# Windowed attention feeding an MoE layer: k of the later batches transposed by DMA, bulk loads tied to product slots, first steps reordered

## The chip, the cores and the metric

One core of a Trainium2 chip runs the whole program. The metric is the device time of one execution in microseconds. The kernel before was run six times: median 354.45 us, lowest 354.02, highest 355.26.

## The reference

Attention over a causal sliding window of 64 keys, for 8 batches of 8 heads with 576 positions of 64 numbers, and then a two-layer block over all 4608 tokens:

```python
scores = scale * np.matmul(q, k.transpose(0, 1, 3, 2))
mask = (rel >= 0) & (rel < window)          # rel = query position - key position
attn = softmax(np.where(mask, scores, -1e9))
attn_out = np.matmul(attn, v)
x = attn_out.transpose(0, 2, 1, 3).reshape(4608, 512)
h = x @ w_in                                 # 512 -> 2048
g = h - np.tanh(h)
out = g @ w_out                              # 2048 -> 512
```

q, k, v and the two weights come as float32, out is float32. The kernel multiplies in bfloat16 and accumulates in float32.

## The kernel before

**Two kinds of work on one in-order TensorE.** The MoE block runs over 9 chunks of 512 tokens. For each chunk `hp_mm` makes 16 tiles of the hidden layer (4 matmuls each, m = 0 to 15), ScalarE takes the tanh, VectorE subtracts (`g_sub`) into gT, and `yp_mm` makes the output from gT and w_out in 16 steps of 4 matmuls, 16 slots later (`LAG`). A slot is one `hp_mm` and one `yp_mm`; it is counted in two half-slots h: an even h holds the hidden product, an odd h the output product. After each group of four output steps `y_out` copies the result out of PSUM on ScalarE and stores it by SyncE. Between these products the attention is placed, pair of heads by pair of heads: g = 4 b + pr is pair pr (0 to 3) of batch b.

**The steps of one pair.** `cast` turns q or k of the pair, which were loaded with 96 groups of six positions on the partitions, into a row layout (GpSimd for most pairs). `tr` transposes the rows on TensorE, six 96x96 blocks each for q and k, into PSUM bank 3 (k of early pairs into bank 2), and copies the result into qT or kT (two buffers each, g modulo 2): q in two halves, by ScalarE and VectorE in the steady part, k in one copy on ScalarE. `scores` makes 9 blocks of 128 keys x 128 columns in three groups of three, each followed by an exp on ScalarE into PT; `masking` multiplies by the mask on VectorE (batches 0 and 1 add the mask by an extra matmul instead); `pv` multiplies by the values in vw; `norm` divides by the row sums on VectorE into xs. When the four pairs of a batch are done, x is transposed into xT, the operand of the MoE product: by TensorE for batches 0 to 2 (`x_tr`), by a transposing DMA on SyncE's queue from batch 3 on (`x_dma`, L251 to L259).

**The values** are loaded (`load_v_all`), cast by GpSimd into vb (`cast_v`, one pair of heads at a time), copied by nine small DMAs per batch from vb into the upper half of vw (`keys_v`, 65 KB each), and shifted into its lower half (`shift_v`, by DMA, or by VectorE for batches 0 and 1). vb is one buffer: a batch's casts wait until the copies of the batch before have landed.

**The loads** of whole batches (`load_all` for q and k, `load_v_all`) are issued by GpSimd, 576 KB each as written, with a cast to bfloat16 on the way; some of batch 0 go pair by pair, on the queues of GpSimd, SyncE or ScalarE (`load`). The weights go on GpSimd's queue too: w_in in three blocks (two of 512 KB, one of 1 MB, `load_w_in`), w_out in four (`load_w_out`).

**What sets the order.** The kernel writes every queue's order out by hand. `PLAN` maps a half-slot h to a script of short steps that `play` issues in that order: `q0a` loads q of pair 0 on ScalarE's queue, `r` does the same for k, `V1`, `K1`, `Q1` load batch 1, `a` and `b` cast q and k, `v` and `d` load and cast values, `k00s` is copy 0 of batch 0's values on SyncE, `z` the shift, `E` and `F` transpose q and k, `R40` is score group 0 of pair 4, `P` the value products with their norm, `M` the mask, `X` x's transpose, `w` and `o` the weight blocks, `n`, `i`, `m` constants. A last letter names the engine (p GpSimd, a ScalarE, v VectorE, s SyncE). The script at -1 is all that comes before the first MoE product. From pair 12 on a loop (L395 to L419) places each step at a half-slot worked out from a (the pair's) and s (the batch's); steps of one half-slot follow the product of that half-slot. Each engine then works through its own list in order, waiting by semaphores; SyncE's list holds value copies, shifts, x's transposes and the output stores, GpSimd's the loads and the casts.

Of the kernel before, what the change touches and what calls it, by code (L numbers as in the profile page):

```python
# [15 lines left out]
def kernel(  # L16
# [26 lines left out]
    const = ctx.enter_context(tc.tile_pool(name="const", bufs=1))  # L43
    qk_pool = ctx.enter_context(tc.tile_pool(name="qk", bufs=2))
    all_pool = ctx.enter_context(tc.tile_pool(name="all", bufs=2))
# [3 lines left out]
    xt_pool = ctx.enter_context(tc.tile_pool(name="xt", bufs=3))  # L49
    g_pool = ctx.enter_context(tc.tile_pool(name="g", bufs=2))  # L50
    psum = ctx.enter_context(tc.tile_pool(name="psum", bufs=1, space=PSUM))

# [3 lines left out]

    ident = const.tile([128, 128], BF16, name="ident")
    seen = const.tile([64, 128], BF16, name="seen")
    mask = ps[:, 5, 480:512].bitcast(BF16)
# [11 lines left out]
    kT = [const.tile([128, 64 + S], BF16, name=f"kt{i}") for i in range(NR)]  # L71
    qT = [const.tile([128, 2, S], BF16, name=f"qt{i}") for i in range(NR)]
    xs = [const.tile([128, NJ, NP, D], BF16, name=f"xs{i}") for i in range(2)]

# [8 lines left out]
    def load(g, n, eng):  # L83

        b, pr = divmod(g, NP)
        if eng is nc.gpsimd:
            if (b, n) not in whole:
                whole[b, n] = all_pool.tile([P, H, E * D], BF16, tag=n, name=n + "all")
            t = whole[b, n][:, pr::NP]
        else:  # L90
            t = qk_pool.tile([P, 2, E * D], F32, tag=n + "f", name=n + "f")
        eng.dma_start(out=t, in_=(q if n == "q" else k)[b, pr::NP].rearrange("h (p e) d -> p h (e d)", e=E))
        stage[g, n] = t

    def load_all(b, n):

        t = all_pool.tile([P, H, E * D], BF16, tag=n, name=n + "all")
        nc.gpsimd.dma_start(out=t, in_=(q if n == "q" else k)[b].rearrange("h (p e) d -> p h (e d)", e=E))
        for pr in range(NP):
            stage[b * NP + pr, n] = t[:, pr::NP]  # L100

    def cast(g, n, eng=nc.gpsimd):
# [59 lines left out]
    def more_constants():  # L162
        nc.vector.memset(qT[1], 0.0)
        nc.vector.memset(kT[1][:, 0:64], 0.0)
        for i in range(2):
            nc.vector.memset(vw[i][0:64, 0], 0.0)

# [25 lines left out]
    def tr(g, which, bank, *engs):  # L193
# [9 lines left out]
        else:  # L203
            move(engs[0], kT[g % NR][:, 64:].rearrange("c (p e) -> c p e", e=E), t)

    def scores(g, grp, bank):
        sp = ps[:, bank, 0:384].rearrange("p (i q) -> p i q", i=3)
        for i in range(3):
            j = 3 * grp + i
            nc.tensor.matmul(sp[:, i, :], kT[g % NR][:, 64 * j:64 * j + 128],  # L210
                             qT[g % NR][:, :, 64 * j:64 * j + 64], start=True, stop=g >= 2 * NP)
            if g < 2 * NP:
                nc.tensor.matmul(sp[:, i, :], ident, hide.rearrange("p h t -> p (h t)"), start=False, stop=True)
# [86 lines left out]
    def at(h, *fn):  # L300
        items.setdefault(h, []).append(fn)
# [13 lines left out]
    def play(script):  # L315
        for step in script.split():
# [50 lines left out]
        -1: """  # L367
            q0a r0s i a0v v00 v02 v03 d02a d00v b0a v01 q1a E0vv r1p d01v r2p m d03p b1v F0a
            k00s q3p k08a a1v R01 F1v R02 E1vv b2a k01p k02a k04a q2p k05s V1 R00 K1 k03s Q1 a2v
            n k06s F2a R10 k07s z0v R12 a3p r3s E2aa P0 d11p d13p w0 R11 w1 E3aa R22 b3a R21  # L370
            b5p w2 Q2 P1 K2 R20 d10p a5p F3v d12a k17s a4p P2 k16s R31 k10s b4p X001v V2 a7p
            k18s R30 b7p o2 k12s k13s X000a R32 b6p P3 o3 k15a X010v X011a E4vv""",
        0: "F4a",
        10: "a6v o0 R40 a9p aAp E5aa k14s b8p F5v a8p R42",
        12: "k11s d20p d22p R41 F6a d21p d23p z1v k25s k27s E6aa R50 P4",
        15: "b9p R52 o1 k24p k22s k20s R51 R61 F7a P5 R62 E7aa",
        19: "R60 F8a k23s R71 P6 k21p k28s X100a k26s R70",
        20: "R72 bBp bAp E8vv",
        23: "X101a P7 z2s R80 E9aa",
        24: "R81",  # L380
        26: "F9a R82 X111a X110a",
        31: "R90 EAvv",
        35: "R92 FAa R91 M8 aBp FBv M9",
        41: "RA2 P9",
        45: "P8 EBaa RA0",
        50: "RA1 X200a MA RB2 RB1 X201v PA RB0",
        56: "MB PB",
# [7 lines left out]
    for g in range(3 * NP, B * NP):  # L395
        b, pr = divmod(g, NP)
        a = 8 * g - 48 - (0, 2, 4)[min(b - 3, 2)]
        s = 32 * b - (0, 2, 4)[min(b - 3, 2)]
        at(a - 7, cast, g, "q")
        at(a - 5, cast, g, "k")  # L400
        at(s - 72 + 5 * pr, cast_v, b, pr)
        at(a, tr, g, "q", 3, nc.scalar, nc.vector)
        at(a + 2, tr, g, "k", 3, nc.scalar)
        for i in range(3):
# [5 lines left out]
        if pr == NP - 1:  # L410
            at(a + 16, x_dma, b)
        for j in range(NJ):
            if pr == 0:
                at(s - 54 + j // 2, keys_v, b, j)
        if pr == 0:
            at(s - 78, load_v_all, b)
            at(s - 64, load_all, b, "q")
            at(s - 63, load_all, b, "k")
            at(s - 47, shift_v, b, 0, NJ - 1)  # L419

# [45 lines left out]
```

## Time and profile before

| what | value |
|---|---|
| median of six runs | 354.45 us |
| the profiled execution | 354.02 us, its span 352.1 us |
| first MoE product starts | 38.67 us |
| last matmul ends | 348.35 us |
| loads of whole batches, issue to landing, median | v 12.0, k 9.7, q 6.4 us |
| moved by DMA | 39.70 MB; read from HBM 36.70 MB, written 9.44 MB |
| x's transposes by DMA | 10, each 1.2 to 5.9 us on SyncE's queue |
| granted TensorE clock | 1.00 |

The profile is of one execution. Its span runs from the first to the last instruction, so some 1.9 us of the execution's time lie outside. "Busy" is time in which an engine executes; PE is TensorE, PEld its weight loads, DVE VectorE, ACT ScalarE, POOL GpSimd, SP SyncE; a name with q (ACTq, SPq) is the engine's sequencer, which issues DMAs. A busy row of the page cuts the span into 40 slices of 8.8 us and gives tenths. In a table by stretch each engine has its busy time and its number of instructions in brackets. A timeline line has start, duration, engine, code line, operation, output and input tiles, and in square brackets how long the engine had been idle and for what it waited.

### The profile page before, as it was taken

Reading aid. Unit: us, or ns where it says so; the run is one execution under the profiler, and the core shown is the slowest. Engines: PE = TensorE matmul, PEld = TensorE weight load, DVE = VectorE, ACT = ScalarE, POOL = GpSimd, SP = SyncE. Lnnn points to the kernel's source line nnn. Section 1 sums busy time; section 2 is a strip of 40 time slices with the busy share of each in tenths; the row PEclk is TensorE's granted clock in tenths of the full one; section 3 lists DMA queues with packets and bytes.
Section 4 is the critical chain, followed back from the end, with each engine's and each line's share of the span. In section 5 each row is a group of like instructions: output and inputs, shape, how many; then the busy total and the mean of one; then the engine's idle time right before and its main releaser. Section 6 shows DMA issues by size and latency. Waiting matters only on the chain.

```text
span 352.1 us, 5822 instructions
## 1 busy us (share of the span) xinstructions
PE 315.6 (90%) x2208; PEld 181.4 (52%) x2239; DVE 204.7 (58%) x322; ACT 195.9 (56%) x356; POOL 104.9 (30%) x138
## 2 busy tenths in 40 slices
PE   0538677999899999999999999999999999999995
PEld 0427356655556555555555555555555444444442
DVE  3617666776676667666667676776776333333400
ACT  3337477955766666666666666666654444444421
POOL 8709625516328318405520642110000000000000
PEclk9999999999999999999999999999999999999999
DMA  8898998749868569965963594244001400010011
GB/s 160 138 207 133 220 209 161 114 102 182 166 118 116 99 136 163 172 141 120 181 115 110 117 156 131 63 100 97 32 31 40 119 30 32 30 60 32 30 77 73
DMA packets 43764, 39.70 MB, mean 113 GB/s; under 512 B 15336, under 2 KB 37672, under 8 KB 43352
## 3 DMA queue, kind: packets, MB, share of 16 engines
q0 software_dynamic: 20432, 17.97, 34.6%
q1 hardware_dynamic: 22600, 20.50, 22.3%
q10 hardware_dynamic: 704, 0.86, 0.8%
q8 instruction: 17, 0.28, 0.3%
q14 instruction: 11, 0.09, 0.1%
HBM read 36.70 MB, written 9.44 MB: 131 GB/s over the span
## 4 chain that ended last, share of the span: by engine, by line
PE 74%; DMA 10%; ACT 5%; DVE 5%; POOL 3%; issue 2%; POOLq 0%; ACTq 0%; DVEq 0%
PE ps L287 33%; PE ps L267 31%; DMA vall<-in_v_dram 6%; DMA vw<-vb 4%; PE ps L224 4%; PE ps L210 3%; PE ps L197 3%; ACT th L271 2%; DVE xs L235 1%; DVE gT L277 1%; ACT pt L214 1%; POOL vb L81 1%; ACT qt L79 1%; POOL vall L112 1%; DVE qt L81 1%
## 5 line engine op out<-in xcount | busy, mean ns | idle before, releaser
L277 DVE TENSOR_TENSOR gT<-ps,th 128x512 bf16<-128x512 f32 x144 | 99.1, 691 | 87.7 <-ACT th L271 84.9
L267 PE MATMUL ps<-xT,wi 128*128 128x512 bf16 x576 | 147.5, 379 | 1.2 <-DVE gT L277 0.9
L287 PE MATMUL ps<-w_out_sb,gT 128*128 128x512 bf16 x545 | 139.9, 379 | 1.8 <-ACT ysb L292 0.2
L271 ACT ACTIVATE th<-ps 128x512 f32<-128x512 f32 x144 | 86.0, 598 | 80.7 <-PE ps L267 80.2
L267 PEld LDWEIGHTS <-wi 128*128 128x128 bf16 x576 | 60.9, 113 | 46.6 <-issue 2.4
L287 PEld LDWEIGHTS <-gT 128*128 128x128 bf16 x576 | 53.6, 98 | 54.1 <-issue 0.5
L214 ACT ACTIVATE pt<-ps 128x384 bf16<-128x384 f32 x96 | 47.0, 491 | 45.9 <-PE ps L210 31.4
L81 POOL COPY vb<-vall 72x1024 bf16<-72x1024 bf16 x28 | 29.3, 1058 | 72.0 <-DMA vw<-vb 51.1
L235 DVE TENSOR_TENSOR xs<-ps,rc 64x576 bf16<-64x576 f32 x64 | 48.3, 755 | 1.5
L210 PE MATMUL ps<-qt,kt 128*128 128x128 bf16 x288 | 36.5, 226 | 9.7 <-ACT pt L214 8.7
L224 PE MATMUL ps<-vw,pt 128*128 128x130 bf16 x288 | 29.6, 223 | 6.4 <-DVE vw L133 3.3
L224 PEld LDWEIGHTS <-pt 128*128 128x128 bf16 x288 | 22.1, 99 | 22.3 <-issue 5.1
L81 POOL COPY qb<-qall 96x768 bf16<-96x768 bf16 x28 | 23.9, 857 | 31.1 <-PE ps L197 16.0
L81 DVE COPY qt<-ps 64x576 bf16<-64x576 bf16 x30 | 22.7, 758 | 14.6 <-ACT qt L79 13.2
L210 PEld LDWEIGHTS <-kt 128*128 128x128 bf16 x288 | 24.6, 102 | 10.4 <-issue 2.4
L81 POOL COPY kb<-kall 96x768 bf16<-96x768 bf16 x28 | 23.2, 831 | 22.0 <-DMA kall<-in_k_dram 10.4
L292 ACT ACTIVATE ysb<-ps 128x512 f32<-128x512 f32 x36 | 21.5, 597 | 14.7 <-PE ps L287 14.7
L79 ACT ACTIVATE qt<-ps 64x576 bf16<-64x576 bf16 x34 | 21.6, 636 | 1.7 <-PE ps L197 1.6
L197 PE MATMUL ps<-ident,qb 96*128 96x96 bf16 x192 | 14.5, 215 | 6.6 <-DVE qb L81 6.2
L79 ACT ACTIVATE kt<-ps 128x576 bf16<-128x576 bf16 x28 | 18.1, 648 | 1.0 <-PE ps L197 1.0
L218 DVE TENSOR_TENSOR pt<-pt,ps 128x1152 bf16<-128x1152 bf16 x24 | 17.9, 744 | 0.4 <-ACT pt L214 0.4
L197 PE MATMUL ps<-ident,kb 96*128 96x96 bf16 x192 | 14.1, 212 | 3.8 <-ACT kb L79 2.8
(48 smaller groups left out, 117.9 us busy)
## 6 DMA issues: line engine op xcount, KB each, us to landing
out_dram<-ysb SPq DMA_DIRECT2D x36, 256.0 KB
vw<-vb SPq DMA_DIRECT2D x65, 65.0 KB
vall<-in_v_dram POOLq DMA_DIRECT2D x7, 576.0 KB, 12.0
kall<-in_k_dram POOLq DMA_DIRECT2D x7, 576.0 KB, 9.7
qall<-in_q_dram POOLq DMA_DIRECT2D x7, 576.0 KB, 6.4
vw<-vw SPq DMA_DIRECT2D x6, 520.0 KB
w_out_sb<-in_moe_w_out_dram POOLq DMA_DIRECT2D x4, 512.0 KB, 19.5
wi<-in_moe_w_in_dram POOLq DMA_DIRECT2D x2, 512.0 KB, 7.2
```

The source lines that it names most:

```text
L79: nc.scalar.activation(o, i, ACT.Copy)
L81: eng.tensor_copy(o, i)
L197: nc.tensor.transpose(tp[:, e, :], src[:, e, :], ident[:P, :P])
L210: nc.tensor.matmul(sp[:, i, :], kT[g % NR][:, 64 * j:64 * j + 128], qT[g % NR][:, :, 64 * j:64 * j + 64], start=True, stop=g >= 2 * NP)
L214: nc.scalar.activation(PT[g % NPT][:, 3 * grp:3 * grp + 3, :], sp, ACT.Exp, scale=scale)
L224: nc.tensor.matmul(ps[:, 5 + grp, 130 * i:130 * i + 130], PT[g % NPT][:, j, :], vw[b % 2][:, j, 2 * pr:2 * pr + 2, :], start=True, stop=True)
L235: nc.vector.tensor_tensor(xo[r, :, :, pr, :], ov[r, :, :, h, 0:D], rc[r].to_broadcast([64, 3, 3, 64]), ALU.mult)
L267: nc.tensor.matmul(hp, w_in_tile(ki, m), chunk_tile(c)[:, :, ki % 2, 64 * (ki // 2):64 * (ki // 2) + 64], start=(ki == 0), stop=(ki == 3))
L271: nc.scalar.activation(th, hp, ACT.Tanh)
L277: nc.vector.tensor_tensor(gT[c][:, m, :], hp, th, ALU.subtract)
L287: nc.tensor.matmul(yp, gT[c][:, m, s * 128:(s + 1) * 128], w_out_sb[:, m, :], start=(m == 0), stop=(m == M - 1))
L292: nc.scalar.activation(ysb, ps[:, yp_bank(c, s), :], ACT.Copy)
```

## The change

k of batches 4 to 7 is no longer transposed by TensorE. GpSimd casts two pairs into one tile (`cast2`), SyncE writes that tile to a buffer in HBM (`bounce`), and SyncE reads it back with a transposing DMA (`tr2`) into kT2, which `scores` reads from pair 16 on. q, k and v of these batches are loaded at half-slots of their own, each after a one-element GpSimd copy (`pace`) that reads gT of the slot before. Pair 12 on is placed 4 half-slots earlier than its plain place, where batch 3 stood at its plain place and batch 4 at 2 earlier. q is cast at a-5 instead of a-7, x's transposing DMA goes out at a+15 instead of a+16, the shift at s-45 instead of s-47. The float32 staging tiles of q and k share three buffers in place of two each. The scripts of `PLAN` are written in another order, in which some steps also change engines (of batch 1's value casts, for example, three go to VectorE and one to GpSimd, where GpSimd had three and ScalarE one), and of the loads k of batch 1 stands later, and k and q of batch 2 stand ahead of the last block of w_in. TensorE has 192 rows fewer (96 transposes and their weight loads).

```diff
-    qk_pool = ctx.enter_context(tc.tile_pool(name="qk", bufs=2))
+    qk_pool = ctx.enter_context(tc.tile_pool(name="qk", bufs=3))
...
+    kT2 = [const.tile([128, 2, 64 + S], BF16, name=f"kt2{i}") for i in range(2)]
...
+    def pace(h):
+
+        c, m = divmod(h // 2 - 1, M)
+        nc.gpsimd.tensor_copy(tick, gT[c][0:1, m, 0:1])
...
     def more_constants():
         nc.vector.memset(qT[1], 0.0)
         nc.vector.memset(kT[1][:, 0:64], 0.0)
+        for i in range(2):
+            nc.vector.memset(kT2[i][:, :, 0:64], 0.0)
...
+    def cast2(g, n):
+
+        if g % 2 == 0:
+            two[n, g // 2] = two_pool.tile([P, E, 2, 2, D], BF16, tag=n, name=n + "b2")
+        nc.gpsimd.tensor_copy(two[n, g // 2][:, :, g % 2].rearrange("p e h d -> p h e d"),
+                              stage.pop((g, n)).rearrange("p h (e d) -> p h e d", d=D))
+
+    def bounce(i, n):
+        t = dram.tile([S, 256], BF16, tag=n, name=n + "d")
+        nc.sync.dma_start(out=t.rearrange("(p e) c -> p (e c)", e=E),
+                          in_=two[n, i].rearrange("p e i h d -> p (e i h d)"))
+        two[n, i] = t
+
+    def tr2(i, n):
+        nc.sync.dma_start(out=kT2[i % 2][:, :, 64:], in_=two.pop((n, i)), transpose=True)
+
     def scores(g, grp, bank):
+        kt = kT[g % NR] if g < 4 * NP else kT2[g // 2 % 2][:, g % 2]
...
-        -1: """
-            q0a r0s i a0v v00 v02 v03 d02a d00v b0a v01 q1a E0vv r1p d01v r2p m d03p b1v F0a
-            k00s q3p k08a a1v R01 F1v R02 E1vv b2a k01p k02a k04a q2p k05s V1 R00 K1 k03s Q1 a2v
-            n k06s F2a R10 k07s z0v R12 a3p r3s E2aa P0 d11p d13p w0 R11 w1 E3aa R22 b3a R21
-            b5p w2 Q2 P1 K2 R20 d10p a5p F3v d12a k17s a4p P2 k16s R31 k10s b4p X001v V2 a7p
-            k18s R30 b7p o2 k12s k13s X000a R32 b6p P3 o3 k15a X010v X011a E4vv""",
-        0: "F4a",
-        10: "a6v o0 R40 a9p aAp E5aa k14s b8p F5v a8p R42",
-        12: "k11s d20p d22p R41 F6a d21p d23p z1v k25s k27s E6aa R50 P4",
-        15: "b9p R52 o1 k24p k22s k20s R51 R61 F7a P5 R62 E7aa",
-        19: "R60 F8a k23s R71 P6 k21p k28s X100a k26s R70",
...
+        -1: """
+            i q0a v00 a0v v02 v03 d02a v01 r2a d01v q3p r0s d00v b0a q1a m r1p d03p F0a E0vv
+            k04a a1v k00s k03s b2a R01 k07p q2p b1v R00 k01p k05s k08s k06s k02a V1 Q1 a2p a3a E1av
+            F1a R10 n R12 r3s R11 K1 z0v R02 E2aa F2v P0 d13v d11p d10v R20 d12v E3aa w0 R22
+            P1 w1 a5p k17s R21 b3a K2 b7p Q2 F3a a4p P2 a7a k18s w2 b4p k13s X000v k12s R31
+            V2 k10s R30 R32 P3 X001a o2 b5p k16s k15a a6a X010v X011v E4vv""",
+        0: "k11s b6p F4a",
+        10: "a8p o3 R40 F5a R42 b8v E5aa",
+        12: "k14s R41 z1v",
+        15: """
+            R52 E6aa o0 R50 F6v o1 d20p P4 b9p R62 R51 F7v d23p a9p R61 d22p aAp d21p k25s E7aa
+            P5 R60""",
+        19: "X100a P6 R70",
...
-        a = 8 * g - 48 - (0, 2, 4)[min(b - 3, 2)]
-        s = 32 * b - (0, 2, 4)[min(b - 3, 2)]
-        at(a - 7, cast, g, "q")
-        at(a - 5, cast, g, "k")
+        a = 8 * g - 48 - (0, 4, 4, 4)[min(b - 3, 3)]
+        s = 32 * b - (0, 4, 4, 4)[min(b - 3, 3)]
+        at(a - 5, cast, g, "q")
+        if b < 4:
+            at(a - 5, cast, g, "k")
+        elif pr % 2 == 0:
+            t = ((14, 11, 5), (19, 16, 10))[pr // 2]
+            at(a - t[0], cast2, g, "k")
+            at(a - t[0] + 1, cast2, g + 1, "k")
+            at(a - t[1], bounce, g // 2, "k")
+            at(a - t[2], tr2, g // 2, "k")
...
-        at(a + 2, tr, g, "k", 3, nc.scalar)
+        if b < 4:
+            at(a + 2, tr, g, "k", 3, nc.scalar)
...
-            at(a + 16, x_dma, b)
+            at(a + 15, x_dma, b)
...
-            at(s - 78, load_v_all, b)
-            at(s - 64, load_all, b, "q")
-            at(s - 63, load_all, b, "k")
-            at(s - 47, shift_v, b, 0, NJ - 1)
+            if b < 4:
+                at(s - 78, load_v_all, b)
+                at(s - 64, load_all, b, "q")
+                at(s - 63, load_all, b, "k")
+            else:
+                for h, f in (s - 79, (load_v_all, b)), (s - 60, (load_all, b, "q")), (s - 67, (load_all, b, "k")):
+                    at(h, pace, h)
+                    at(h, *f)
+            at(s - 45, shift_v, b, 0, NJ - 1)
```

## The prediction

> **What bounds the kernel now.** I read the page's busy rows first, then the busy times by stretch, then TensorE's timeline in a steady stretch and the queues of the first 60 us, last the chain of waits there.
>
> ```profile
> PE 315.6 (90%) x2208; PEld 181.4 (52%) x2239; DVE 204.7 (58%) x322; ACT 195.9 (56%) x356; POOL 104.9 (30%) x138
> PE   0538677999899999999999999999999999999995
> DMA  8898998749868569965963594244001400010011
> ```
>
> Two regimes: TensorE (PE) is full from about slice 10 on, and the DMA engines are full in the first seven slices (60 us). By stretch (width, then busy time and count of each engine, clock, DMA share, GB/s):
>
> ```profile
> 0.00:38.60 38.60, 16.45 (x180) 13.81 (x181) 19.22 (x36) 15.73 (x26) 25.64 (x44) 1.00 0.96 164
> 38.60:60.00 21.40, 16.73 (x166) 10.92 (x164) 14.10 (x22) 15.33 (x31) 8.63 (x12) 1.00 1.15 204
> 60.00:80.00 20.00, 18.49 (x162) 11.82 (x163) 14.86 (x23) 14.43 (x31) 9.04 (x12) 1.00 0.60 108
> 120.00:140.00 20.00, 19.84 (x148) 11.50 (x148) 13.84 (x22) 13.13 (x26) 9.46 (x12) 1.00 0.80 144
> 140.00:260.00 120.00, 118.19 (x863) 67.99 (x875) 82.10 (x128) 77.10 (x141) 32.01 (x38) 1.00 0.59 116
> ```
>
> Seen: 118.2 of 120 us busy where the later batches run, 16.7 of 21.4 after the first MoE product (38.67 us). In the full stretch the timeline gives the price of one set of k transposes:
>
> ```profile
> 229.51 1.03 PE L267 MATMUL ps<-xT,wi 128*128 128x512 bf16 x4
> 230.39 0.41 PE L197 MATMUL ps<-ident,kb 96*128 96x96 bf16 x6
> 230.64 1.03 PE L287 MATMUL ps<-w_out_sb,gT 128*128 128x512 bf16 x4
> 231.51 1.03 PE L267 MATMUL ps<-xT,wi 128*128 128x512 bf16 x4
> ```
>
> From the product at 229.51 to the next at 230.64 are 1.13 us; without transposes between (230.64 to 231.51) 0.87. So one set costs 0.26 us of a full engine.
>
> In the start, batch 0's values are the chain. Each value copy (vw from vb) goes through a crowded DMA:
>
> ```profile
> 13.34 0.63 ACTq L127 DMA_DIRECT2D vw<-vb  x1
> 19.46 0.61 ACTq L127 DMA_DIRECT2D vw<-vb  x1
> 20.12 0.49 ACT L214 ACTIVATE pt<-ps 128x384 bf16<-128x384 f32 x1 [5.83 <-DMA vw<-vb]
> ```
>
> ScalarE's (ACT's) second copy waits for the completion of an earlier one, issued at 9.84 on SP, until 19.46, with exps queued behind it. It lands about 25.8 (the second shift on VectorE, DVE, starts at 25.78), so the first value products finish only at 27.1. GpSimd (POOL) is held just as long:
>
> ```profile
> 26.58 2.05 POOL L81 COPY vb<-vall 72x1024 bf16<-72x1024 bf16 x2 [10.69 <-DMA vall<-in_v_dram]
> 28.57 1.52 POOL L142 DMA_DIRECT2D wi<-in_moe_w_in_dram  x2
> ```
>
> and the chain of waits goes on through batch 1's copies, up to the shift before P4:
>
> ```profile
> 34.45 7.20 DMA vw<-vb
> 41.67 7.89 DMA vw<-vb
> ```
>
> [...] the trace has x's transposes, 18 blocks a batch:
>
> ```profile
> 238.00:240.00 2.00, 2.00 (x18) 1.10 (x16) 1.80 (x3) 1.47 (x3) 0.00 (x0) 1.00 0.33 66
> 240.00:242.00 2.00, 2.00 (x15) 1.10 (x14) 1.29 (x3) 1.35 (x3) 0.00 (x0) 1.00 0.96 186
> 242.00:244.00 2.00, 2.00 (x17) 1.10 (x15) 0.64 (x2) 1.09 (x2) 0.00 (x0) 1.00 0.58 175
> ```
>
> Issued at 237.72 and 238.99, all done before 244, beside a 256 KB store[...]. [...] the transposing read waits on SP until the bounce has landed.
>
> **The change part by part.** The sum is made against the profiled execution: 354.02 us, span 352.1; the median of six runs is 0.43 more.
>
> *k of batches 4 to 7 by DMA.* Removed: 16 sets, 96 transposes with their weight loads, 16 x 0.26 = 4.2 us of PE where it is full; and 16 ACT copies of 0.648 us, worth nothing (ACT is 64% busy there). The 16 GpSimd casts stay (about 0.83 us each). Added on SP: 8 bounces at about 0.6 us and 8 transposes at about 1.35 us of issue, 16 us in all over some 130. Queued behind them: value copies and output stores; the stores have three buffers and one is due per 8 half-slots (8.45 us), so a hold of a few us costs nothing. DMA time: k is as large as x, so about 3 us of the engines per batch, plus the bounce, in a stretch at share 0.59. Deadline: k is loaded at s-67, cast at s-62, bounced at s-59, transposed at s-53, and its scores stand at s-43; a half-slot is 1.03 us. A load of this kind lands in 6.1 us (q, issued alone first) to 9.7 (k behind q). With 9.7: landed s-57.5, cast s-56, bounce landed about s-52 (0.6 of issue and some 3), transposed about s-48 (4 us, from the rows above). Five half-slots of cover are left; if that goes, PE waits by the excess, four times. Bounds for the transpose: 3 us[...]; I take 4. Pairs 2 and 3 have five half-slots more.
>
> *The GpSimd step.* Twelve one-element copies, about 0.1 us each (a one-column memset takes 0.10): nothing beside a GpSimd at 30%. It adds a wait on VectorE's product of the slot before; behind it stand the load and the casts of v, q and k. q is loaded at s-60, first cast due s-53, transposed s-48: at 6.1 us landed by s-54, 12 half-slots to use. v, 8.6 to 10.2 us, is due at s-72 after s-79, so its cast waits some 2 us; the copies it feeds come at s-54. Cost 0; bound 2 us a batch if q comes as slowly as k.
>
> *Later attention moved 2 to 4 half-slots earlier:* the same work on a full in-order engine: 0.
>
> *First steps.* Batch 0's last ACT copy no longer waits for a copy just issued but for q's second load, of about 7.4 us. Against that, the constants now stand ahead of the first q copies on VectorE (memsets 0.54 + 0.09 + 2 x 0.09 + 1.04, about 1.9 us), so first scores start near 13.3 instead of 10.6. Two exps later the copy goes out at about 15.4, 4 us sooner; with its 6.3 us it lands at 21.7. Then VectorE takes three value casts of batch 1, behind batch 1's load: issued near 12.3 and, at 14.7 us, landing near 27. Two casts at 0.7, and P1's scaling starts near 28.4 instead of 30.03; the first product comes about 2 us earlier. Batch 1's value copies can then start near 29.5 instead of 34.2, and P4 stands after two products more, so its 1.25 us wait goes. Sum about -3. Bounds: -6 (all 4 us come through, and half of the 4.7 us idle from 38.6 to 60), and +4: the last w_in block is now queued behind k's and q's loads of batch 2. It went at 30.84 and landed in 13.2; those two, standing where it will stand, landed at 50.0 and 53.7. It is needed at half-slot 16, 56.9 us before and some 53 after.
>
> Sum: 354.02 - 4.2 - 3.0 = 346.8; with 0.43, 347.3.
>
> **The rivals.** *Only k's saving comes through*: the start is held by transfers of the same bytes at share 0.96 to 1.15, so its order is worth nothing: 354.45 - 4.2 = 350.3. For it: that share; against it: the 6 us completion wait, which is order alone.
> *They cancel*: the w_in block late by 4 us at half-slot 16: 354.3. Against it: the same DMA queue also gets rid of a load moved back.
> *Slower, by late k*: the transpose out of DRAM is slow[...]. PE waits there in order, everything behind it. It decides from (4.2 + 3.0)/4 = 1.8 us per batch[...]. I put it at 358. For it: no transpose from DRAM is in this trace. Against it: x's 18 blocks in about 6 us.
> *A start that gains 6 or more*: 344 and below.
>
> **Chances.** An expected size 0.48 (347.3, own range 344 to 349.5), k only 0.22, cancelled 0.08, late k 0.16, larger gain 0.06. A measurement of this kernel tells 0.2% (0.7 us) from no change. Faster 0.77, same 0.06, slower 0.17. The range 344 to 355 leaves out late k and half of the larger gain.
>
> **What would show it.** After 140 us: no k transposes, a period per pair of 8.2 instead of 8.45 us, TensorE still full. In the waits: score products waiting for kt2's DMA would be the slower rival. In the start: the second ACT copy near 15, the first product near 36.5, a wait of products for wi at half-slot 16 if the block is late. I am wrong if the first product comes no earlier, or if the stretch after 140 us has new gaps.

## The result, and the profile after

The changed kernel is slower by about 1%: median 359.72 us against 354.59 for the kernel before on the same chip, ratio 1.0103 (95% interval 1.0075 to 1.0131). The forecast was 347.3, range 344 to 355. The profiled execution of the changed kernel took 364.19 us (span 362.2) and is one of its slower ones: they spread from 354.6 to 364.7 us, one of 1847 aside, and ratios leave out those over 1.5% above a kernel's fastest, so a ratio can be lower than the medians suggest.

The page of the changed kernel, the rows that answer to those of before:

```profile
PE 317.3 (88%) x2112; PEld 180.7 (50%) x2143; DVE 204.2 (56%) x327; ACT 192.9 (53%) x343; POOL 100.8 (28%) x144
PE   0368788799899998989987998979999999999995
PEclk9999899999999999999999899989999999999999
DMA  8899999759856997798959896976100410010012
```

The transposes are gone, but PE is busier in time than before (317.3 against 315.6 us), and in the later slices, where it had only nines, there are eights and sevens. The clock row (PEclk, the clock that TensorE was granted) drops to eight in two of these slices and in one at the start; where it was 0.50, four matmuls of a hidden product took 1.91 us (at 40.06) instead of 1.03 (at 50.17), so that fewer of them can be busy for longer. At the start one of the scores took 0.31 us instead of 0.22, up to 35.6 us here and up to 29.2 before, at a granted clock given as 1.00 up to 38 us; why is not shown. The DMA row is higher in many of the later slices. By stretch (width, busy time and count of PE, PEld, DVE, ACT and POOL, clock, DMA share, GB/s), 110 to 250 us of the kernel before, then of the changed one:

```profile
110.00:250.00 140.00, 138.04 (x1006) 79.48 (x1021) 96.48 (x150) 90.56 (x167) 46.86 (x56) 1.00 0.66 126
```
```profile
110.00:250.00 140.00, 128.82 (x864) 71.64 (x879) 89.44 (x139) 78.29 (x144) 50.05 (x68) 0.98 0.85 151
```

In the same 140 us PE is busy 9.2 us less, and the DMA engines are busy at 0.85 instead of 0.66. (The share adds up the times of packets; where they overlap it comes out above 1, as 1.15 from 38.6 to 60 us in the kernel before.) TensorE's timeline of the changed kernel names the stops (in brackets the idle time and what ended it):

```profile
162.56 0.43 PE L209 MATMUL ps<-ident,qb 96*128 96x96 bf16 x6 [0.99 <-POOL qb L86]
...
188.61 0.43 PE L209 MATMUL ps<-ident,qb 96*128 96x96 bf16 x6 [0.99 <-POOL qb L86]
198.90 0.43 PE L209 MATMUL ps<-ident,qb 96*128 96x96 bf16 x6 [1.94 <-POOL qb L86]
...
226.85 0.43 PE L209 MATMUL ps<-ident,qb 96*128 96x96 bf16 x6 [1.56 <-POOL qb L86]
237.93 0.66 PE L209 MATMUL ps<-ident,qb 96*128 96x96 bf16 x6 [2.73 <-POOL qb L86]
```

All five are transposes of q that wait for GpSimd's cast, 8.2 us together. GpSimd's own timeline says for what the cast waits, here for the last batch:

```profile
213.25 1.05 POOL L86 COPY vb<-vall 72x1024 bf16<-72x1024 bf16 x1 [11.14 <-DMA vall<-in_v_dram]
...
215.01 0.18 POOL L110 COPY tick<-gT 1x1 bf16<-1x1 bf16 x1
215.13 0.78 POOL L103 DMA_DIRECT2D kall<-in_k_dram  x1
...
224.20 0.82 POOL L224 COPY kb<-kall 96x768 bf16<-96x768 bf16 x1 [7.24 <-DMA kall<-in_k_dram]
...
227.63 0.77 POOL L103 DMA_DIRECT2D qall<-in_q_dram  x1
...
237.04 0.82 POOL L86 COPY qb<-qall 96x768 bf16<-96x768 bf16 x1 [7.58 <-DMA qall<-in_q_dram]
```

v's cast waits 11.14 us for v's load; k's load stands behind it. k's cast waits 7.24 us for k's load; q's load stands behind that. q is issued at 227.63 and PE wants it at 235.2 (237.93 less 2.73), so q has 7.6 us and not the twelve half-slots of the plan. Only the stops at 198.90 and 237.93 wait for q's own load in this way. Those at 188.61 and 226.85 are for q of the batch before, which has long been loaded: its cast stands behind k's, while that waits for k's load (5.01 us the first time, 7.24 here). The ticks themselves hardly wait.

**The sum**, for the profiled execution, whose span is 10.1 us longer. The first product comes 1.4 us later. From it to the last matmul's end are 309.7 us before (38.67 to 348.33) and 318.3 after (40.06 to 358.41), 8.7 more. Stops of PE from 105 to 262 us are 10.8 us against 1.0: +9.8. The granted clock was lower from 200 to 204 and from 236 to 242, worth 3.4 us (width by missing clock): +3.4. k's saving: -4.2. Together 9.0. Left out are the 1.7 us that the clock is worth from 38 to 44, where PE also stands idle in both kernels. The median is only 5.1 us longer; which of these terms are smaller in the shorter executions is not known, as there is one trace.

### The profile page after: what moved, and what is told of

Same layout as the page of the kernel before. It is cut to its first block, busy times and chain, and to the rows that moved or that the text cites. A ratio compares the mean times of both kernels' runs of the same rounds, so it can differ in the third digit from the quotient of the medians.

```text
span 362.2 us, 5618 instructions
## 1 busy us (share of the span) xinstructions
PE 317.3 (88%) x2112; PEld 180.7 (50%) x2143; DVE 204.2 (56%) x327; ACT 192.9 (53%) x343; POOL 100.8 (28%) x144
## 4 chain that ended last, share of the span: by engine, by line
PE 63%; DMA 11%; issue 9%; SPq 5%; ACT 4%; POOL 4%; DVE 4%; POOLq 0%; DVEq 0%; ACTq 0%
PE ps L318 26%; PE ps L298 25%; DMA vw<-vb 4%; SPq L137 4%; PE ps L241 3%; PE ps L255 3%; DMA qall<-in_q_dram 3%; PE ps L209 2%; DMA vw<-vw 2%; ACT pt L245 2%; DMA vall<-in_v_dram 1%; ACT th L302 1%; POOL vb L86 1%; DVE xs L266 1%; POOL qb L86 1%
## 5 line engine op out<-in xcount | busy, mean ns | idle before, releaser
L298 PE MATMUL ps<-xT,wi 128*128 128x512 bf16 x576 | 149.6, 384 | 1.1 <-DVE gT L308 1.1
L318 PE MATMUL ps<-w_out_sb,gT 128*128 128x512 bf16 x545 | 141.5, 382 | 2.0 <-issue 0.2
L245 ACT ACTIVATE pt<-ps 128x384 bf16<-128x384 f32 x96 | 47.1, 491 | 47.5 <-PE ps L241 35.6
L241 PE MATMUL ps<-qt,kt 128*128 128x128 bf16 x288 | 37.7, 232 | 10.0 <-DVE qt L86 5.4
L86 POOL COPY vb<-vall 72x1024 bf16<-72x1024 bf16 x26 | 27.4, 1058 | 65.1 <-DMA vall<-in_v_dram 55.2
L86 POOL COPY qb<-qall 96x768 bf16<-96x768 bf16 x26 | 22.1, 856 | 41.1 <-DMA qall<-in_q_dram 22.9
L86 DVE COPY qt<-ps 64x576 bf16<-64x576 bf16 x26 | 19.7, 757 | 20.3 <-ACT qt L84 20.0
L84 ACT ACTIVATE qt<-ps 64x576 bf16<-64x576 bf16 x38 | 24.2, 638 | 8.6 <-PE ps L209 8.2
L209 PEld LDWEIGHTS <-qb 96*128 96x128 bf16 x192 | 12.2, 105 | 15.3 <-POOL qb L86 10.6
L224 POOL COPY kb<-kall 96x768 bf16<-96x768 bf16 x16 | 13.0, 828 | 21.2 <-DMA kall<-in_k_dram 21.2
L209 PE MATMUL ps<-ident,kb 96*128 96x96 bf16 x96 | 8.0, 229 | 11.1 <-ACT kb L84 10.8
```

The source lines that it names most:

```text
L84: nc.scalar.activation(o, i, ACT.Copy)
L86: eng.tensor_copy(o, i)
L209: nc.tensor.transpose(tp[:, e, :], src[:, e, :], ident[:P, :P])
L241: nc.tensor.matmul(sp[:, i, :], kt[:, 64 * j:64 * j + 128], qT[g % NR][:, :, 64 * j:64 * j + 64], start=True, stop=g >= 2 * NP)
L245: nc.scalar.activation(PT[g % NPT][:, 3 * grp:3 * grp + 3, :], sp, ACT.Exp, scale=scale)
L298: nc.tensor.matmul(hp, w_in_tile(ki, m), chunk_tile(c)[:, :, ki % 2, 64 * (ki // 2):64 * (ki // 2) + 64], start=(ki == 0), stop=(ki == 3))
```

## The experiments

**Theories after the result.** (A) the pacing or the late q load does it, an order that can be mended. (B) k's new path does it through its DMA traffic: whichever transfer has least cover (time between its issue and the moment it is needed, beyond what it takes) comes late. (C) the forecast's slower rival, scores that wait for the transposed k. (D) the new start costs. In what follows, "the kernel before" has ratio 1, and times are compared with its runs on the same chip (353.9 to 354.6 us).

**1. The changed kernel without the tick.**

```diff
-                    at(h, pace, h)
```

> The changed kernel without the one-element step (the pace); loads stand where they stood. Order theory (what delays q is that its load stands on GpSimd behind the casts that wait for k, not the step's own wait, which is 1.1 us once in the changed kernel): the gaps of TensorE before q's transposes stay, 8 us in all between 140 and 240 us, and the time is within 1.5 us of the changed kernel, about 358. Pace theory (the step holds the loads back): the gaps go and the time is 349 to 351. Traffic theory (k's bounce and transposes slow all loads): as the order theory, about 358.

Measured: 360.62 us, ratio 1.0116 (1.0086 to 1.0146). Pacing is not the cause. PE also stopped 4.9 us in two for x's transposes, which it had not done with the tick, and 5.1 us instead of 8.2 for q's casts.

**2. q's load right behind k's.**

```diff
-(s - 60, (load_all, b, "q")), (s - 67, (load_all, b, "k"))
+(s - 66, (load_all, b, "q")), (s - 67, (load_all, b, "k"))
```

> The changed kernel with one move: q's load of batches 4 to 7 at s-66, straight behind k's (s-67), instead of s-60. Order theory: q no longer waits behind the casts that wait for k, lands some 5 us earlier, the gaps before q's transposes fall from 8 us to under 2 and the clock stays at 1.00 there; 348 to 351. Traffic theory: the loads are slow because of the transposes, q lands late in any order; gaps over 5 us, 356 or more.

Measured: 361.6 us, ratio 1.0174 (1.0122 to 1.0226). The stops before q went, and others came: 1.59 and 4.14 us before products that wait for x's transposes, 0.70 and 1.09 for V's shift. Mending q's order does not make it faster; nor do the other orders of the changed kernel (numbers 8, 14, 15 and 17). That is against theory A.

**3. k by DMA alone.** The kernel before with cast2, bounce, tr2 and kT2, k's load at s-67, nothing paced, the old plan.

```diff
+            at(a - t[0], cast2, g, "k")
+            at(a - t[0] + 1, cast2, g + 1, "k")
+            at(a - t[1], bounce, g // 2, "k")
+            at(a - t[2], tr2, g // 2, "k")
...
-        at(a + 2, tr, g, "k", 3, nc.scalar)
+        if b < 4:
+            at(a + 2, tr, g, "k", 3, nc.scalar)
...
-            at(s - 63, load_all, b, "k")
+            at(s - 63 if b < 4 else s - 67, load_all, b, "k")
```

> The kernel before with one part of the change: k of batches 4 to 7 cast in pairs, bounced and transposed by DMA at the change's half-slots, with k's load moved from s-63 to s-67, ahead of q's at s-64; no pace, first steps as before. Order theory: the saving of 16 x 0.26 us comes through, 350 to 351. Traffic theory: TensorE gets gaps in the later batches as in the changed kernel, 355 or more.

Measured: 366.99 us, ratio 1.035 (1.0307 to 1.0394): the part that was to save 4.2 us costs 12. Its chain of waits, and two of its stretches of 2 us:

```profile
138.78 12.04 DMA xT<-xs
...
150.87 1.89 PE ps L291 x4
```
```profile
146.00:148.00 2.00, 0.00 (x0) 0.00 (x0) 0.47 (x1) 0.11 (x1) 1.67 (x2) 1.00 1.27 190
...
152.00:154.00 2.00, 2.00 (x6) 0.73 (x5) 0.57 (x1) 0.60 (x1) 0.87 (x2) 0.50 0.54 149
```

In the kernel before:

```profile
139.41 5.09 SPq L256 DMA_TRANSPOSE xT<-xs  x2
```

x's transposes are issued at 138.78 and land 12 us later; PE has nothing at all from 146 to 148 (5.77 us in all), then runs at half clock. In the kernel before they went out at 139.41 and PE did not wait. The same happens again at 226 us. No score waits for kT2.

**4. The new plan alone.** The kernel before with the changed kernel's scripts and shared staging buffers.

> The kernel before with one part of the change: the first steps in the changed order (with the three shared staging buffers). The start theory says that they cost some 1.5 us (first product at about 40 instead of 38.7[...]): 355.5 to 357. Its rival says that the start is held by transfers and its order is worth nothing: 354 to 355.

Measured: 354.16 us, ratio 0.9992 (0.9973 to 1.0011). The first steps are worth nothing, either way: theory D falls, and with it the forecast's -3. The first product came at 38.30 here, so the changed kernel's 40.06 is not the new order alone.

**5. The traffic alone.** Number 3, but the scores read the k that PE transposes (from the same cast, whose tile has three buffers here and one in number 3) and kT2 is read by nobody.

```diff
-        kt = kT[g % NR] if g < 4 * NP else kT2[g // 2 % 2][:, g % 2]
...
-        if b < 4:
-            at(a + 2, tr, g, "k", 3, nc.scalar)
+        at(a + 2, tr, g, "k", 3, nc.scalar)
```

> The kernel before with k's new path added and not used: k of the later batches is cast two pairs at a time, stored to HBM and transposed by the DMA engines on SP's queue, with the loads where k by DMA alone had them (k at s-67, q at s-64), but the scores still read the k that TensorE transposes. So the reading of kT2 is taken out and all its traffic and all its issues on SP stay. Theory (the traffic or SP's queue delays x's transposes): as slow as k by DMA alone or slower, since PE keeps its 4.2 us of transposes, 365 to 371 us (ratio 1.03 to 1.045), with PE gaps of about 5 us before products that wait for x's transposes near 150 and 226 us. Rival (a late transposed k holds the scores): 354 to 357 us (ratio under 1.01), since no score reads it.

Measured: 364.13 us, ratio 1.0299 (1.0232 to 1.0366). Nothing depends on the added transfers, and it is as slow as number 3:

```profile
145.47 0.33 PE L236 MATMUL ps<-qt,kt 128*128 128x128 bf16 x3
154.10 1.89 PE L293 MATMUL ps<-xT,wi 128*128 128x512 bf16 x4 [8.30 <-DMA xT<-xs]
```

One stop of 8.30 us for x's transposes, with the half clock after it (worth 3.4 us), covers the whole difference. That is theory B, and against C as the cause of the loss. It does not tell the transfers' time on the DMA engines from the time that their issue holds SP's queue, which also moves the loads: k's and q's went out at 137.07 and 138.81 here, right ahead of x's transposes at 139.49, and at 132.50 and 134.25 in number 12.

**6. k's stores and transposes on ACT's queue.**

```diff
-        nc.sync.dma_start(out=kT2[i % 2][:, :, 64:], in_=two.pop((n, i)), transpose=True)
+        nc.scalar.dma_start(out=kT2[i % 2][:, :, 64:], in_=two.pop((n, i)), transpose=True)
```

> k by DMA alone, with its 8 stores to HBM and 8 transposes issued by ACT instead of SP. If SP's queue is the cause (k's issues of 1.3 to 2.7 us hold V's copies, so GpSimd's casts of V, so the loads behind them, which then run beside x's transposes), SP's queue is as before, K's and q's loads are issued near 134.5 us again, x's transposes land within 8 us and the time is 350 to 357 us (ACT pays about 15 us of issues, in its idle third). If the time of the DMA engines is the cause, x's transposes still land 12 us after their issue and the time stays at 362 to 368 us.

Measured: 369.0 us, ratio 1.0428 (1.0369 to 1.0487). Inconclusive on what it was made for: ACT stood behind the issue of its own transposes (3.68 us at 135.24, for example), and PE's largest stops are now for ACT's output copies, 6.8 of 16.3 us, and SP's waits list x's transposes held for kt, 33.4 us in four waits, so the two queues' transposes did not run side by side. Placed like this, a second queue is no way out. The DMA share from 138 to 142 was 1.54, against 1.05 in number 3.

**7. The paced loads alone**, on the kernel before.

```diff
+            at(s - 63, load_all, b, "k")
+            else:
+                for h, f in (s - 79, (load_v_all, b)), (s - 60, (load_all, b, "q")), (s - 67, (load_all, b, "k")):
+                    at(h, pace, h)
+                    at(h, *f)
```

> The kernel before with the paced loads alone (V at s-79, K at s-67, q at s-60, each behind the small GpSimd step), k still transposed on TensorE. If k's path is the cause of the loss, the paced loads cost little by themselves: 352 to 356 us (ratio 0.993 to 1.005), perhaps with small gaps before q's transposes. If the late q load is the cause of the loss in the changed kernel, 358 to 361 us (ratio 1.01 to 1.02) with gaps of 1 to 3 us before q's transposes in the later batches.

Measured: 354.28 us, ratio 1.0008 (0.9986 to 1.003). Late loads at these places cost nothing as long as k's traffic is not there: q's load at s-60 landed in 6.4 us (median of the stretch), with k's traffic in 8.5; here k's casts, at a-5, do not stand ahead of it. Numbers 4 and 7 clear two of the three large parts of the change, on the kernel before. The changed kernel with k back on TensorE was not run.

**8. All loads earlier in the changed kernel** (V at s-84, K at s-76, q at s-72).

> The changed kernel with all three bulk loads earlier, still paced: V at s-84, K at s-76, q at s-72. Theory (a bulk load that runs beside x's transposes and k's is what makes one of them late): with the loads 8 half-slots or more ahead of their use and away from the copies, q's gaps vanish; if x's transposes then land within 8 us the time is 349 to 354 us (ratio 0.985 to 1.0). Rival (the traffic of k costs wherever the loads are): the wait moves to x's transposes or to the copies of V again, 358 to 362 us.

Measured: 360.09 us, ratio 1.0166 (1.0115 to 1.0216). The stops before q are gone, and PE waits 6.3 us for x's transposes instead, whose issue on SP took up to 11.98 us for two.

**9. k's second transpose behind x's**, in number 3.

```diff
-            t = ((14, 11, 5), (19, 16, 10))[pr // 2]
+            t = ((14, 11, 5), (19, 16, 3))[pr // 2]
```

> k by DMA alone (k by DMA alone before: ratio 1.035), with the second transpose of each batch issued 7 half-slots later, so that SP issues it behind x's two transposes instead of 2 half-slots ahead of them. If the nearness of that transpose is what makes x's late, x's transposes land some 6 us after their issue as in the kernel before, the two PE gaps of 5.8 us go, and the time is 350 to 355 us (ratio 0.99 to 1.003). If it is the DMA engines' time in the whole stretch, x's transposes stay late or V's copies or the late k take their place: 359 to 367 us (ratio 1.012 to 1.035).

Measured: 361.33 us, ratio 1.0178 (1.0133 to 1.0224), half of the loss of number 3. Nearness matters, but x still came late, with 10.2 us of stops in the profiled execution (366.64 us): at 138.27 and 140.02 GpSimd issued k's and q's loads, with x's transposes between them at 139.79.

**10 and 11. Half of k**: the first two pairs of each batch by DMA (no k transpose next to x's), or the last two.

```diff
+        dma = b >= 4 and pr < 2
+        if not dma:
             at(a - 5, cast, g, "k")
```

> k by DMA alone for the first two pairs of each later batch, the other two transposed on TensorE as before. So half of k's traffic, and no transpose of k next to x's. If the nearness is the cause: no loss, half of the PE saving, 351 to 355 us (ratio 0.991 to 1.002). If the engines' time in the stretch is the cause, about half of the loss: 358 to 361 us (ratio 1.012 to 1.02).

> k by DMA alone for the last two pairs of each later batch, the first two on TensorE: half of k's traffic, all of it next to x's transposes. If the nearness is the cause: nearly the whole loss, 362 to 368 us (ratio 1.02 to 1.037). If the engines' time in the stretch is the cause: half of the loss, 358 to 361 us (ratio 1.012 to 1.02), the same as with the other half.

Measured: 1.0021 (0.9975 to 1.0067; median 358.37 us) and 1.0092 (1.0065 to 1.0119; 360.03 us). By the ratios half of the traffic costs much less than half of the 3.5%, and more where it stands next to x's; by the medians, 4.0 and 5.7 us above the kernel before, it costs a third and nearly a half of number 3's 12.7, and the first ratio rests on four executions. The medians lie where the engines' time was expected to put them, the ratios below that (1.012 to 1.02), so nearness is not told clearly from amount here. The traces show two ways to a late x. With the first half, k's transpose at 122.32 holds V's copies on SP, k's and q's loads go out at 136.33 and 138.08, next to x's transposes (139.66), and PE stops 3.51 us. With the last half the loads are early (132.36 and 134.10), but k's transpose at 131.68 takes 5.92 us of SP, and PE stops 5.49 us. Neither is a gain.

**12. The stores alone**: number 5 without tr2.

```diff
-            at(a - t[2], tr2, g // 2, "k")
```

> The kernel before with k's stores to HBM alone: the two-pair casts and the 8 stores of 288 KB are there, no DMA transposes k, and TensorE transposes k as before (the full unused traffic gave 1.030). If the transposes are what costs: 353 to 357 us (ratio 0.997 to 1.007). If the stores cost as much as the transposes: 358 to 361 us (ratio 1.012 to 1.02). It also has the casts of two pairs and k's load at s-67, so at no loss those are cleared too.

Measured: 356.24 us, ratio 1.0016 (0.9993 to 1.0038). The bounce to HBM, the casts of two pairs and k's load at s-67 cost nothing that the ratio can tell, though the median of all 22 executions is 1.9 us above the kernel before; the 2.8% between this and number 5 belong to the transposes, with what their issue holds up.

**13. Loads on x's transposes, no DMA of k**: number 7 with q's load at s-71 and k's at s-70.

> The kernel before with no DMA of k transposed: the paced loads alone, but q's and k's put at s-71 and s-70, right on x's transposes (s-72), where they came in k by DMA alone. If bulk loads beside x's transposes are enough to hold PE, x's transposes land late by some 3 to 6 us and the time is 358 to 364 us (ratio 1.01 to 1.03). If k's transposes are needed for it, x's issue takes 5 to 8 us as it did beside loads before, PE waits under 2 us a batch, and the time is 353 to 357 us (ratio 0.997 to 1.007).

Measured: 361.45 us, ratio 1.0185 (1.0159 to 1.021). So k's transposes are not needed for the stop:

```profile
150.27 1.90 PE L272 MATMUL ps<-xT,wi 128*128 128x512 bf16 x4 [6.34 <-DMA xT<-xs]
```

The loads went out at 134.34 and 135.22, x's transposes at 137.62, 3 us behind them; in the kernel before it was 4 to 5 us (134.53, 135.29, 139.41), and in number 7 q's load stood 8 us behind x's (k 138.40, x 139.50, q 147.81). From 146 to 150 the engines were busy at 1.41 and moved 119 GB/s; in the kernel before, from 138 to 146, 1.24 to 1.27 moved 207 to 247. The packets held the engines longer and moved less; why is open. In the two later batches loads and x met too (179.66 and 180.08), and PE did not wait: the whole loss is from one meeting.

**14. Everything kept apart** in the changed kernel.

```diff
-            t = ((14, 11, 5), (19, 16, 10))[pr // 2]
+            t = ((8, 5, 0), (19, 14, 3))[pr // 2]
...
-(s - 79, (load_v_all, b)), (s - 60, (load_all, b, "q")), (s - 67, (load_all, b, "k"))
+(s - 84, (load_v_all, b)), (s - 63, (load_all, b, "q")), (s - 66, (load_all, b, "k"))
```

> The changed kernel with everything that the DMA engines do for a batch kept apart as far as the slots allow: V's load at s-84, K's at s-66, q's at s-63 (x's transposes are at s-72), k's first store and transpose at s-53 and s-48, the second behind x's at s-46 and s-35, and k's first casts late enough not to hold GpSimd in front of q's load. If order and nearness are what cost, no gap over 1 us in the later batches and 349 to 353 us (ratio 0.985 to 0.997). If the DMA engines are simply too full in this stretch (0.66 of their time before, 0.88 with k's traffic), something is late again and it is 356 to 362 us (ratio 1.005 to 1.02).

Measured: 368.18 us, ratio 1.0369 (1.0323 to 1.0416). x's transposes now go out in 2.6 to 2.9 us and never hold PE. The wait has moved to k itself: four stops for kt, 12.8 us (2.33, 5.66, 2.78 and 2.06). k's transposes stand 5 and 7 half-slots later than in the changed kernel, with 5 and 8 left to their scores, and the four that PE waited for landed 7.2 to 11.2 us after their issue. It is slower than either expectation, and no test of room alone: it took k's own cover away.

**15. q behind k, and k's second transpose behind x's.**

> The changed kernel with two moves only: q's load right behind k's (s-66), which by itself moved the waits from q to x and V (ratio 1.017), and k's second transpose behind x's (7 half-slots later), which by itself halved the loss of k by DMA alone. If the two causes add, 352 to 356 us (ratio 0.993 to 1.005), with x's transposes issued within 5 us. If the stretch is simply too full, 357 to 362 us.

Measured: 368.94 us, ratio 1.0396 (1.0351 to 1.0442), also slower than either expectation. The same happens: 11.9 us of stops for kt, the longest 6.80.

**16. The changed kernel with half of k** (as number 10).

> The changed kernel with k by DMA for the first two pairs of a batch only, the other two transposed on TensorE: half of the PE saving, half of k's traffic, none of it next to x's transposes. In a stretch that is too full, half the traffic costs much less than half: 351 to 356 us (ratio 0.99 to 1.005), q's gaps under 1 us. If the loss is in proportion to the traffic: 357 us (ratio 1.005 to 1.01).

Measured: 358.56 us, ratio 1.0081 (1.0051 to 1.011). q's stops 4.7 us in two, about half of the changed kernel's 8.2: of the two expectations, loss in proportion to the traffic is the one that came, though the ratio cannot be told from the changed kernel's own 1.0103.

**17 and 18. The last places tried**, with all of k and with half.

```diff
-            t = ((14, 11, 5), (19, 16, 10))[pr // 2]
+            t = ((11, 8, 3), (19, 16, 10))[pr // 2]
...
-(s - 79, (load_v_all, b)), (s - 60, (load_all, b, "q")), (s - 67, (load_all, b, "k"))
+(s - 84, (load_v_all, b)), (s - 62, (load_all, b, "q")), (s - 66, (load_all, b, "k"))
```

> The changed kernel with all of k by DMA, k's second transpose back in its place ahead of x's (behind x's it made k itself late), V's load at s-84, K's at s-66, q's at s-62 ahead of k's first casts (now s-59), k's first store and transpose at s-56 and s-51. If there is an order in which all of this traffic fits, no gap over 1 us and 349 to 353 us (ratio 0.985 to 0.997). If the DMA engines are too full for k's whole traffic, the wait is at x's, q's, V's or k's again and it is 356 to 362 us (ratio 1.005 to 1.02).

> The same with k by DMA for the first two pairs of a batch only (half of the traffic, and no k transpose near x's), V's load at s-84, K's at s-67, q's at s-64, which takes q's load out from behind k's casts: the two gaps before q's transposes, 4.7 us together in the last such run, should go. That gives 350 to 354 us (ratio 0.987 to 0.999), the PE saving of 2.1 us and nothing against it. If half of the traffic is already too much, a wait shows up elsewhere and it is 356 to 359 us.

(The half has q at s-64 and k at s-67.) Measured: 361.17 us, ratio 1.0196 (1.0152 to 1.0239), and 355.71 us, ratio 1.0057 (1.0032 to 1.0082). With all of k x, q and V are in time, and k is late twice:

```profile
168.82 0.50 PE L241 MATMUL ps<-qt,kt 128*128 128x128 bf16 x3 [3.65 <-DMA kt<-kd]
```

With half, k was late too, 3.7 us in three stops. No version here beats the kernel before.

**What they say together.**

| kernel | k by DMA | DMA queue of SP, 110 to 250 us | PE's stops, 105 to 262 us | most of it for | ratio |
|---|---|---|---|---|---|
| before | none | 33.4% | 1.0 us | - | 1 |
| 7, paced loads | none | 33.4% | 2.1 | x | 1.0008 |
| 12, stores only | none | 41.2% | 2.4 | a product of VectorE | 1.0016 |
| 18 | half | 45.6% | 4.9 | k | 1.0057 |
| changed kernel | all | 50.8% | 10.8 | q | 1.0103 |
| 17 | all | 56.0% | 8.9 | k | 1.0196 |
| 5, traffic only | all, unused | 52.7% | 9.3 | x | 1.0299 |
| 3, k alone | all | 53.9% | 13.3 | x | 1.035 |
| 14, kept apart | all | 47.3% | 14.4 | k | 1.0369 |

The queue's column is the time of its packets as a share of all 16 engines. With all of k in it, each order has some transfer late, and the order chooses which; no order with all of k is better than the changed kernel's own (number 1, 1.0116, cannot be told from it). That amount, and not place alone, is the limit rests on eight orders (numbers 1, 2, 3, 8, 9, 14, 15, 17) that all lose; it is not shown that none exists that doesn't. The column does not order the ratios either: number 14, with 47.3%, loses most of those listed. Place counts by itself as well (numbers 9, 11 against 10, and 13).

## Why the prediction was wrong, point by point

**The PE saving was right.** In the changed kernel's stretches without a stop the period per pair is what was said:

```profile
144.55 1.52 DVE L266 TENSOR_TENSOR xs<-ps,rc 64x576 bf16<-64x576 f32 x2
152.73 1.52 DVE L266 TENSOR_TENSOR xs<-ps,rc 64x576 bf16<-64x576 f32 x2
160.91 1.52 DVE L266 TENSOR_TENSOR xs<-ps,rc 64x576 bf16<-64x576 f32 x2
```

VectorE's last step of successive pairs comes every 8.18 us, foreseen 8.2; before 8.45 (202.36, 210.81, 219.26). The 4.2 us exist; they are overspent.

**The step that failed is the DMA time of k's path**: "k is as large as x, so about 3 us of the engines per batch, plus the bounce, in a stretch at share 0.59", costed at nothing for everybody else. What the runs showed in its place: the same traffic with nobody waiting for it costs 2.99% (number 5), and 0.16% without its transposes (number 12). Two things are wrong with the step. Its size: SP's queue went from 33.4% (before) to 41.2% with the stores and 52.7% with the transposes. Of 140 us these are 10.9 and 16.1 us of all 16 engines, for four batches: 2.7 us of store and 4.0 us of transpose each, 6.8 in all (packets that overlap are all counted in this, and the last window holds two output stores fewer, so it is a rough size). The stretch from 110 to 250 was at 0.66, not 0.59 (which took in the quiet time after the last load), and came to 0.85. And its kind: a mean share below 1 was read as room. The transfers come in clumps; before, the share was already 1.24 to 1.27 for 8 us where x's transposes ran, and x was needed some 6 us after its issue. I asked whether k's own transpose would be in time, and never who would be late because of it.

**The 4 us for a transpose** were taken from x's transposes in a quiet stretch (237.72, done before 244); at 203.92 the kernel before already had two that took 7.27 us of SP's queue instead of 2.76. Beside bulk loads two such transposes took 12.0 us to land at 138.78 and 14.7 at 211.69 (number 3). Number 13 shows a price in time for two loads next to x's transposes: 1.0185, against 1.0008 with one of them elsewhere (number 7).

**The hold on SP** ("queued behind them: value copies and output stores ... costs nothing") was too narrow. The transposing reads did wait there for their stores (14.9 us in three waits, the longest 5.6, in the changed kernel). In number 3 one k transpose took 2.65 us of SP at 121.45 with seven V copies behind it; GpSimd's cast of V, which waits for those copies, came at 134.76 instead of 131.01, and behind it k's and q's loads at 136.52 and 138.26 instead of 134.53 and 135.29, onto x's transposes at 138.78. This chain is read from the traces; what it alone is worth was not measured.

**The GpSimd step**: the tick was right at 0 (numbers 1 and 7). "12 half-slots to use" for q failed: GpSimd works in order, k's cast (s-62) stands ahead of q's load (s-60) and waited 7.24 us for k's load, so q had 7.6 us, and q itself took 8.5 instead of 6.1. The forecast's own figures held the first half of this: with k landed at s-57.5, GpSimd stands at k's cast from s-62 to there, and q's load and casts stand behind it; it reckoned q from s-60 all the same. The bound written for it, 2 us a batch, is what came: 8.2 us in four batches.

**First steps, -3**: came to 0 (number 4), and the changed kernel's first product came at 40.06, not near 36.5. Some single steps were right: ACT's second copy went out at 15.48 (foreseen 15.4), batch 1's copies at 29.89 (29.5), P4's wait is gone. P1's scaling started at 30.03 as before, not at 28.4: the three casts of batch 1 on VectorE came only at 28.73, behind P0's scaling. And the early copy landed no earlier, as VectorE's second shift shows in the changed kernel (before 25.78):

```profile
15.48 0.62 ACTq L137 DMA_DIRECT2D vw<-vb  x1
```
```profile
25.53 0.70 DVE L143 COPY vw<-vw 64x2080 bf16<-64x2080 bf16 x1 [1.23 <-DMA vw<-vb]
```

4 us sooner out, 0.25 us sooner in: the forecast had added the old duration to the new start. That the bytes of the start set it (share 1.03 before and after in the first 60 us) is the likely reading; it was not tried apart. The argument of the rival "only k's saving comes through" was right on this half.

**Late k**, the slower rival: right sign, wrong mechanism for this kernel. No score waited for kT2 in the changed kernel or in number 3; it does in numbers 14, 15, 17 and 18, where k's transposes stand later. There they landed 7.2 to 11.6 us after their issue (14, 15 and 17); the forecast had taken 4. How slow a transpose from DRAM could be no trace had shown, and the rival's 358 us was an estimate of mine with no trace behind it.

**Later attention earlier: 0** was not tried by itself; nothing in the traces speaks against it. It is also less than the text ahead of the forecast says: `(0, 4, 4, 4)[min(b - 3, 3)]` is 0 for batch 3 and 4 from batch 4 on, so only batch 4 moves, by 2 half-slots.

## What to carry to other kernels

An operation moved from a full engine to the DMA engines can be paid by whatever other transfer has the least cover (x's transposes, for which PE stood 8.30 us in number 5), so list every transfer with a deadline near the new ones, with its issue, landing and consumer, before calling the traffic free. Read the DMA share in stretches of 2 to 4 us around these deadlines, not as a mean of 100: 0.66 on the mean held clumps of 1.24 to 1.27. To find out what traffic costs, add it and let nobody read it (number 5): one run tells it from a late result. And where an in-order engine issues loads and also does casts that wait for loads, reckon each load from the end of the waits ahead of it (7.24 us for k's cast ahead of q's load in the changed kernel).

## What was not expected of the hardware

- Transposing DMAs beside bulk loads: two that took 2.76 us of SP's queue at 237.72 in the kernel before, with no load beside them, took 8.38 us of it at 138.78 and 13.71 at 211.69 in number 3 beside loads, with a DMA share of 1.0 to 1.4 from 138 to 148. It is not so each time: at 172.66 the kernel before had two beside k's load that took 2.73 us, at a share of 1.27 from 172 to 174.
- PE's clock after a stop: 0.50 after stops of 1.94 and 2.73 us (changed kernel), 5.77 (number 3) and 7.45 (number 9), 1.00 after 0.99 and 1.56 (changed kernel) and 2.33 (numbers 14 and 18). So the length of the stop alone does not tell which was followed by half clock (1.94 was, 2.33 was not; short idle times of PE before them are not counted). By the missing clock each such stretch is worth 1.7 us (both of the changed kernel) or 3.4 (both of number 3), which at 0.50 is 3.4 or 6.8 us of width, an estimate from these sums. In number 3 the two are worth 6.8 us together, half as much as its stops.
